# Attention scores in quarters of TensorE's array, and later places for the products behind them

## Chip, core and metric

One core of one Trainium2 chip runs the kernel alone. The metric is the device time of one execution in microseconds (us), taken as the median over runs. Engines are called by the profile's names: PE is TensorE's matmul, PEld its weight loads (they overlap PE), DVE is VectorE, ACT ScalarE, POOL GpSimd, SP SyncE, which starts most transfers.

## What is computed

Attention over pooled keys and values, then a mixture of experts on the rows that it gives. B = 8, H = 8, S = 576, D = 64; eight keys are pooled into one, so there are 72 pooled keys (SP in the kernel). The 4608 rows x of 512 go through a skip score, eight experts' gates and one expert each.

```python
k_p = k.reshape(B, H, Sp, pool, D).mean(axis=3)
v_p = v.reshape(B, H, Sp, pool, D).mean(axis=3)
scores = scale * np.matmul(q, k_p.transpose(0, 1, 3, 2))
scores = scores - np.max(scores, axis=-1, keepdims=True)
attn = np.exp(scores)
attn = attn / (np.sum(attn, axis=-1, keepdims=True) + 1e-09)
x = np.matmul(attn, v_p)            # then (B * S, H * D)
do_compute = x @ w_skip > 0         # other rows are left as x
e_idx = np.argmax(x @ w_gate, axis=1)
out = x + softmax(x @ w_gate)[e_idx] * (np.maximum(x @ w1[e_idx], 0) @ w2[e_idx])
```

## The kernel before

**Tiles.** The attention part takes 36 tiles (NT) of 128 tokens. All its matmuls are float32, and each shows as two instructions in the profile. A batch has four and a half tiles, so tiles 4, 13, 22 and 31 lie across two batches; they use matmuls on 64 output columns at a time, one half for each batch. Queries lie with two heads on the 128 partitions (64 dimensions each), so four head pairs make a tile. `scores` (L303) takes a pair's 128x128 block of queries as weights and streams 144 columns of `kbd`, a block-diagonal array: one head's 72 keys on the upper 64 partitions, the other's on the lower, zeros elsewhere. One half (two pairs, four heads) fills one bank of PSUM, `sc`.

**One iteration t** is a stage of a software pipeline over tiles, written out by hand; each engine works its instructions off in this order.

- ACT copies tile t−2's turned probabilities from PSUM (`turned_p`, L328, 128x640) and, where a new batch comes in, its turned pooled values (`turned_v`, L267).
- DVE normalises tile t−3 (`normal`: reciprocal L355, gates' part L359, rows L360, logits L362); the rows are stored by SP.
- PE computes the scores of tile t (L303). DVE takes the minimum of each head's (negated) scores (`softmax`, L309), ACT the eight exponentials (L315).
- With a new batch PE multiplies its turned values by the gates' weights (`gates_pe`, L278), and DVE spreads them over the arrays of values later in the iteration (`gates_dve`, L281, L284): so the value matmuls give the gates' logits beside the rows.
- PE runs route products if a group has them ready (`routes.products`, L397 to L401), then the values of tile t−2 (`values`, L341 and L344) into `o`, two banks that have one buffer, and turns tile t−1's exponentials (`turn_p`, L323, L324) into `pt`.
- DVE and ACT take further work from lists within a budget of time per iteration; POOL takes its own (sums of values, low halves of weights, memsets, and the table writes of routed groups, L415, one for each tile, an indirect transfer).

**Routing** goes in groups of 9, 5, 4, 6, 5, 4 and 3 tiles. A group's steps are a generator: DVE steps, ACT's exponentials (L394), PE's products, DVE's ranks and payments, then POOL's table writes. `routes.held` is set while a group stands before its exponentials or products.

**Behind the attention** PE goes on, from 147.0 us, with 128x512 and 128x384 matmuls of one expert's two layers on nine tiles of rows ("near" tokens: L532 to L534 for the first layer, L550 to L552 for the second). A list fixes PE's order there: 28 of the 32 steps of the first layer, then the transposes L1072 of rows that POOL gathers from the table (L1040) once all table writes are done, then the rest. Next comes the experts' part, in which PE is busy to the end.

```python
sc = [scores(t, i) for i in range(2)]
mn = softmax(t, sc)
if new is not None:
    gates_pe(new)
routes.products()
exponentials(t, sc, mn)
os_[t - 2] = values(t - 2, pts.pop(t - 2))
turn_p(es.pop(t - 1))
if new is not None:
    gates_dve(new)
```

## Time and profile before

| what | value |
|---|---|
| median of 3 runs | 480.49 us (479.95 to 480.7) |
| the profiled execution | 481.24 us, of which 479.2 us are the profile's span |
| granted clock of TensorE, mean | 0.999 |
| PE, PEld busy | 463.5 us, 417.1 us |
| DVE, ACT, POOL busy | 303.4 us, 225.7 us, 250.3 us |
| attention's last value matmuls on PE | 147.0 us |

The span runs from the first to the last instruction that the profile has; 2.04 us of the execution lie around it. Times within the trace count from the start of the span. Busy time is the sum of an engine's instructions, and a matmul's end is modelled, so that neighbours overlap. The granted clock is 1.00 where TensorE runs at 2.4 GHz and .50 where it runs at 1.2.

### The profile page before, as it was taken

What the parts mean: (1) busy time and instruction counts of PE and PEld (TensorE: products, weight loads), DVE (VectorE), ACT (ScalarE), POOL (GpSimd) and SP (SyncE); (2) the same over time, 40 slices, a digit from 0 to 9 for tenths busy, and PEclk for the clock granted to TensorE, in tenths of its full rate; (3) what the DMA queues carried; (4) which work ended last, traced back from release to release, by engine and by line L of the source; (5) the groups of instructions that cost most, each with busy time, mean ns of one, the idle gap of its engine ahead of it and who ended that gap; (6) DMA issues with size and microseconds to landing.
All of it is one profiled execution on the core that took longest, in us unless ns stands there. A gap on an engine that the chain in (4) does not pass through costs nothing. (4 is left out here: it accounts for less than half of the span.)

```text
span 479.2 us, 11182 instructions
## 1 busy us (share of the span) xinstructions
PE 463.5 (97%) x3043; PEld 417.1 (87%) x3044; DVE 303.4 (63%) x713; ACT 225.7 (47%) x578; POOL 250.3 (52%) x328
## 2 busy tenths in 40 slices
PE   7999999999999999899999999999999999999995
PEld 4799899989999979798989987989899898989894
DVE  5877888798788622578795667663846554343321
ACT  5678768888891211546462645612435251212110
POOL 4499499999998154363342424362624161515242
PEclk9999999999999999999999999999999999999999
DMA  8999999996931026679787497877687223322021
GB/s 278 388 396 390 361 352 332 384 333 207 328 122 68 11 62 215 230 228 308 247 289 244 136 290 241 300 240 251 202 256 262 89 95 101 129 66 88 22 88 42
DMA packets 52042, 103.88 MB, mean 217 GB/s; under 512 B 10031, under 2 KB 22959, under 8 KB 50336
## 3 DMA queue, kind: packets, MB, share of 16 engines
q1 hardware_dynamic: 40544, 78.18, 47.8%
q0 software_dynamic: 11456, 25.22, 15.0%
q8 instruction: 17, 0.28, 0.2%
q14 instruction: 25, 0.20, 0.1%
HBM read 80.85 MB, written 31.21 MB: 234 GB/s over the span
## 5 line engine op out<-in xcount | busy, mean ns | idle before, releaser
L1289 POOL DMA_INDIRECT out<-ring,slot x33 | 35.8, 1085 | 109.3 <-POOLq L1115 105.6
L315 ACT ACTIVATE e<-sc,mn 128x72 f32<-128x72 f32 x288 | 65.0, 345 | 7.4 <-DVE mn L309 6.8
L1527 ACT ACTIVATE hhi<-psl 128x256 fp32r<-128x256 f32 (+3 forms) x59 | 23.5, 400 | 94.0 <-ACTq L1115 93.5
L1384 PE MATMUL psl<-xlo,w1hi 128*128 128x256 f32 (+3 forms) x220 | 64.1, 291 | 0.0
L1383 PE MATMUL psl<-xhi,w1hi 128*128 128x256 f32 (+3 forms) x220 | 64.0, 291 | 0.0
L1385 PE MATMUL psl<-xhi,w1lo 128*128 128x256 f32 (+3 forms) x220 | 64.0, 291 | 0.0
L1284 POOL DMA_INDIRECT ring<-out,slot x42 | 46.6, 1109 | 22.6 <-issue 22.4
L341 PE MATMUL o<-vbd,pT 128*128 128x148 f32 (+1 forms) x312 | 49.4, 298 | 1.1 <-DVE x L360 1.1
L1626 DVE SCALAR_TENSOR_TENSOR hlo<-psl,hhi 128x256 fp32r<-128x256 f32 (+2 forms) x55 | 23.2, 423 | 41.3 <-DVEq L1115 39.0
L415 POOL DMA_INDIRECT table<-pay,r_di x36 | 36.7, 1018 | 12.6 <-DVE mb L443 6.4
L1383 PEld LDWEIGHTS psl<-xhi,w1hi 128*128 128x128 f32 x220 | 41.3, 188 | 0.8 <-issue 0.4
L1384 PEld LDWEIGHTS psl<-xlo,w1hi 128*128 128x128 f32 x220 | 41.3, 188 | 0.5
L341 PEld LDWEIGHTS o<-vbd,pT 128*128 128x128 f32 (+1 forms) x312 | 38.6, 179 | 3.6 <-ACT ring L213 1.0
L1385 PEld LDWEIGHTS psl<-xhi,w1lo 128*128 128x128 f32 x220 | 41.2, 187 | 0.0
L1297 POOL DMA_DIRECT2D sorted<-ring x39 | 22.2, 572 | 32.9 <-DMA ring<-out,slot 25.8
L1603 DVE TENSOR_TENSOR w2lo<-stage,w2hi 128x1024 fp32r<-128x1024 f32 x28 | 34.3, 1223 | 6.6 <-DVEq L1115 6.4
L1384 PE MATMUL psd<-xlo,w1hi 128*128 128x256 f32 (+3 forms) x132 | 38.4, 291 | 0.0
L1385 PE MATMUL psd<-xhi,w1lo 128*128 128x256 f32 (+3 forms) x132 | 38.4, 291 | 0.0
L1383 PE MATMUL psd<-xhi,w1hi 128*128 128x256 f32 (+3 forms) x132 | 38.4, 291 | 0.0
L1409 PE MATMUL mb<-w2hi,hlo 128*128 128x512 f32 x88 | 34.8, 396 | 0.0
L1409 PE MATMUL psf<-w2hi,hlo 128*128 128x512 f32 x88 | 34.8, 396 | 0.0
L1407 PE MATMUL psf<-w2hi,hhi 128*128 128x512 f32 x88 | 34.8, 395 | 0.0
(276 smaller groups left out, 1216.0 us busy)
## 6 DMA issues: line engine op xcount, KB each, us to landing
stage<-in_w SPq DMA_DIRECT2D x64, 512.0 KB, 5.5
sorted<-ring POOLq DMA_DIRECT2D x39, 256.0 KB, 3.3
out<-x SPq DMA_DIRECT2D x36, 256.0 KB, 5.4
stage<-in_k SPq DMA_DIRECT2D x6, 1152.0 KB, 8.8
blocks<-sorted SPq DMA_DIRECT2D x100, 64.0 KB
qt<-in_q SPq DMA_DIRECT2D x9, 512.0 KB, 7.4
hhi<-in_vm SPq DMA_DIRECT2D x4, 1024.0 KB, 7.7
hlo<-in_vm SPq DMA_DIRECT2D x3, 1024.0 KB, 9.8
```

Of the source, the lines that this page charges most:

```text
L315: nc.scalar.activation(ev[:, h // 2, k0:k0 + SP], sc[:, h * SP:(h + 1) * SP], AF.Exp, bias=mn[:, 4 * i + h:4 * i + h + 1], scale=-1.0)
L341: nc.tensor.matmul(o_[sl, g * 2 * VA:(g + 1) * 2 * VA], pT[:, 2 * a + g, sl], vbd[b % 2][:, 2 * a + g, :], start=(g == 0), stop=False)
L415: m = nc.gpsimd.indirect_dma_start(table, bass.IndirectOffsetOnAxis(ap=di[:, j:j + 1], axis=0), flat(fin["pays"][:, t0 + j:t0 + j + TW // ...
L1284: g.indirect_dma_start(ring[:, (s + 3) % 9, 0:D], None, out, bass.IndirectOffsetOnAxis(ap=slot[:, s:s + 1], axis=0), bounds_check=NTOK - 1 ...
L1289: g.indirect_dma_start(out, bass.IndirectOffsetOnAxis(ap=offsets, axis=0), ring[:, (s + 3) % 9, 0:D], None, bounds_check=NTOK - 1, oob_is_ ...
L1383: t.matmul(ps, whi[0][:, k, w], xhi[:, k, xs], start=(k == 0), stop=False)
L1384: t.matmul(ps, whi[0][:, k, w], xlo[:, k, xs], start=False, stop=False)
L1385: last = t.matmul(ps, wlo[0][:, k, w], xhi[:, k, xs], start=False, stop=(k == 3))
L1407: t.matmul(ps, hhi[:, k, sl], whi[1][:, k, :], start=(k == 0), stop=False)
L1409: last = t.matmul(ps, hlo[:, k, sl], whi[1][:, k, :], start=False, stop=(k == 7))
L1527: a.activation(hhi[:, f, xs], bank(f, xs, alone), AF.Relu).then_inc(sem["act"], 1)
L1603: v.tensor_tensor(chunk_of(wlo, c), chunk_view(stage[c], c), chunk_of(whi, c).bitcast(F32), ALU.subtract).then_inc(sem["wlo1" if c < 4 els ...
```

## The change

From tile 3 on the scores are computed in quarters: for each of four head pairs, each half of the tokens (64 weight columns) and each head (64 rows of the array) one matmul with 72 moving columns, 16 instead of 4 in the program (32 instructions in the profile instead of 8). The zeros of `kbd` are no longer read. The heads on the upper 64 rows go to one bank, those on the lower to the other; minimum and exponentials take the heads in that order. Tiles 0 to 2 keep the old form. The turned probabilities go to two banks and are copied in two instructions, 128x384 and 128x256. The gates' product on PE moves behind the values, and its spreading on DVE into the next iteration, ahead of the minimum. Route products that become ready in the iteration itself go behind the values from tile 15 on (PICKED), and DVE then takes one more route step instead of filling its budget; those that stood ready when the iteration began stay in front of the values. Of a group's last four DVE steps the two for payments now come before the two for ranks.

```diff
@@ scores, exponentials
-        def scores(t, half):
+        def by_halves(t):
+            return t < 3
+
+        def scores_by_halves(t, half):
             sc = ps_s.tile([128, 512], F32, name="sc")[:, 0:4 * SP]
             for g in range(2):
-                for sl, b in parts(t):
-                    nc.tensor.matmul(sc[sl, g * 2 * SP:(g + 1) * 2 * SP], qts[t // QG][:, t % QG, half * 2 + g, sl],
-                                     kbd[b % 2][:, half * 2 + g, :], start=True, stop=True)
+                nc.tensor.matmul(sc[:, g * 2 * SP:(g + 1) * 2 * SP], qts[t // QG][:, t % QG, half * 2 + g],
+                                 kbd[0][:, half * 2 + g, :], start=True, stop=True)
             return sc
 
+        def scores(t):
+            if by_halves(t):
+                return [scores_by_halves(t, i) for i in range(2)]
+            sc = [ps_s.tile([128, 512], F32, name="sc")[:, 0:4 * SP] for _ in range(2)]
+            for g in range(4):
+                for i, sl in enumerate(halves):
+                    b = (t * 128 + i * 64) // S
+                    for r, o in zip(halves, range(2)):
+                        nc.tensor.matmul(sc[o][sl, g * SP:(g + 1) * SP], qts[t // QG][r, t % QG, g, sl],
+                                         kbd[b % 2][r, g, o * SP:(o + 1) * SP], start=True, stop=True)
+            return sc
+
-        def exped(e, sc, mn, i):
-            ev = e[:, (4 * SP + GAP) * i:(4 * SP + GAP) * i + 4 * SP].rearrange("p (k g) -> p g k", g=2)
-            for h in range(4):
-                k0 = (h % 2 ^ i) * SP
-                nc.scalar.activation(ev[:, h // 2, k0:k0 + SP], sc[:, h * SP:(h + 1) * SP], AF.Exp,
-                                     bias=mn[:, 4 * i + h:4 * i + h + 1], scale=-1.0)
+        def exped(e, sc, mn, n, halved):
+            for j in range(4):
+                g, o = (2 * n + j // 2, j % 2) if halved else (j, n)
+                i = g // 2
+                ev = e[:, (4 * SP + GAP) * i:(4 * SP + GAP) * i + 4 * SP].rearrange("p (k g) -> p g k", g=2)
+                k0 = (o ^ i) * SP
+                nc.scalar.activation(ev[:, g % 2, k0:k0 + SP], sc[:, j * SP:(j + 1) * SP], AF.Exp,
+                                     bias=mn[:, 4 * n + j:4 * n + j + 1], scale=-1.0)
@@ turned probabilities
         def turn_p(e):
...
-                    nc.tensor.transpose(ptf[:, (2 * i + g) * 128:(2 * i + g) * 128 + 128], ev[:, g], ident)
-            nc.tensor.transpose(ptf[:, 512:640], e[:, 256:384], ident)
+                    nc.tensor.transpose(pt[:, i, (2 * i + g) * 128:(2 * i + g) * 128 + 128], ev[:, g], ident)
+                if i == 0:
+                    nc.tensor.transpose(pt[:, 0, 256:384], e[:, 256:384], ident)
 
         def turned_p():
-            pT = ap.tile([128, 5, 128], F32, name="pT")
-            nc.scalar.activation(flat(pT), ptf[:, 0:640], AF.Copy)
+            pT = [ap.tile([128, 3 - i, 128], F32, name=f"pT{i}") for i in range(2)]
+            for i, sl in enumerate((slice(0, 384), slice(256, 512))):
+                nc.scalar.activation(flat(pT[i]), pt[:, i, sl], AF.Copy)
             return pT
@@ values: the first half reads pT[0], the second pT[1] and the left columns pT[0]
-                        nc.tensor.matmul(o_[sl, g * 2 * VA:(g + 1) * 2 * VA], pT[:, 2 * a + g, sl], vbd[b % 2][:, 2 * a + g, :],
+                        nc.tensor.matmul(o_[sl, g * 2 * VA:(g + 1) * 2 * VA], pT[a][:, g, sl], vbd[b % 2][:, 2 * a + g, :],
...
-                    nc.tensor.matmul(ov[sl, :, 1, :], pT[:, 4, sl], vl4[b % 3][:, 2 * a:2 * a + 2, :], start=False, stop=True)
+                    nc.tensor.matmul(ov[sl, :, 1, :], pT[0][:, 2, sl], vl4[b % 3][:, 2 * a:2 * a + 2, :], start=False, stop=True)
@@ route
-            for a, b in zip(ranked, paid) if last else zip(paid, ranked):
+            for a, b in zip(ranked, paid) if last else (paid, ranked):
@@ Queue.products
             def products(self):
+                had = bool(self.held)
                 while self.held:
                     self.step(True)
+                return had
@@ the iteration
+            known = routes.held
             routes.exponentials()
             if t > 2:
                 normal(t - 3)
-                sc = [scores(t, i) for i in range(2)]
+                if t - 1 in turns:
+                    gates_dve(turns[t - 1])
+                sc = scores(t)
...
-            if new is not None:
-                gates_pe(new)
...
+            elif known or t < PICKED:
+                routes.products()
             else:
-                routes.products()
+                routes.exponentials()
             spent = act.take(t, 0.4 if new is not None else 0.0, 1)
             exponentials(t, sc, mn)
             os_[t - 2] = values(t - 2, pts.pop(t - 2))
+            if new is not None:
+                gates_pe(new)
+            fresh = t < NT - 1 and routes.products()
...
-            if new is not None:
-                gates_dve(new)
...
             while t < NT - 1 and busy < (DVE if t < PICKED else DVEL) and routes.step():
-                busy += 0.24
+                busy += 9 if fresh else 0.24
```

PE's order in the iteration of tile 9, the first of batch 2, before (`sc` scores, `o` values, `mb` gates, `pt` turned probabilities):

```order
L303 MATMUL sc<-ring,qt 128x144 x4
L278 MATMUL mb<-wgs,vT 128x36 x3
L341 MATMUL o<-vbd_121,pT 128x148 x2
L344 MATMUL o<-vl_123,pT 128x2x74
L341 MATMUL o<-vbd_121,pT 128x148 x2
L344 MATMUL o<-vl_123,pT 128x2x74
L323 MATMUL pt<-cfs,e_126 128x128 x4
L324 MATMUL pt<-cfs,e_126 128x128
```

and the same place in the change:

```order
L317 MATMUL sc<-ring,qt 64x72 x16
L359 MATMUL o<-vbd_121,pT_712 128x148 x2
L362 MATMUL o<-vl_123,pT_712 128x2x74
L359 MATMUL o<-vbd_121,pT_713 128x148 x2
L362 MATMUL o<-vl_123,pT_712 128x2x74
L278 MATMUL mb<-wgs,vT 128x36 x3
L339 MATMUL pt<-cfs,e_126 128x128 x2
L341 MATMUL pt<-cfs,e_126 128x128
L339 MATMUL pt<-cfs,e_126 128x128 x2
```

The gates' three matmuls stand behind the values, and the transpose of the left columns has moved to the middle of its five.

DVE's order at the entry of the same batch, before (`lg` logits, `mn` minimum, `vbd` and `vl` the spread gates, `kp` pooled keys, `rc` and `x` normalisation):

```order
L362 TENSOR_REDUCE lg<-l_635 128x9
L309 TENSOR_REDUCE mn<-sc 128x4 x2
L281 TENSOR_TENSOR vbd_120<-mb,cfs 128x8x9
L284 TENSOR_TENSOR vl_124<-mb,cfs 96x4x9
L208 TENSOR_REDUCE kp<-stage 128x72
L355 RECIPROCAL rc<-o 128x8
L359 TENSOR_TENSOR l_688<-o,rc 128x72
L360 TENSOR_TENSOR x<-o,rc 128x512
L362 TENSOR_REDUCE lg<-l_688 128x9
L309 TENSOR_REDUCE mn<-sc 128x4 x2
```

and in the change:

```order
L323 TENSOR_REDUCE mn<-sc 128x4 x2
L208 TENSOR_REDUCE kp<-stage 128x72
L373 RECIPROCAL rc<-o 128x8
L377 TENSOR_TENSOR l_784<-o,rc 128x72
L378 TENSOR_TENSOR x<-o,rc 128x512
L380 TENSOR_REDUCE lg<-l_784 128x9
L281 TENSOR_TENSOR vbd_120<-mb,cfs 128x8x9
L284 TENSOR_TENSOR vl_124<-mb,cfs 96x4x9
L323 TENSOR_REDUCE mn<-sc 128x4 x2
```

The two multiplications stand one normalisation later, directly ahead of the next tile's minimum. On POOL one memset and one table write change places; SP's order is the same.

## Rows read from the trace of the kernel before

**Rows 1.** The page: busy time, share of the span and instructions of each engine.
```profile
PE 463.5 (97%) x3043; PEld 417.1 (87%) x3044; DVE 303.4 (63%) x713; ACT 225.7 (47%) x578; POOL 250.3 (52%) x328
```

**Rows 2.** Busy us by stretch: stretch, length, PE, PEld, DVE, ACT, POOL (instructions), granted clock, DMA, GB/s.
```profile
17.00:55.70 38.70, 37.69 (x318) 35.59 (x318) 30.48 (x90) 29.15 (x107) 26.79 (x37) 1.00 1.02 393
55.70:156.00 100.30, 98.04 (x820) 92.58 (x819) 83.41 (x302) 75.30 (x252) 92.20 (x108) 1.00 0.76 266
```

**Rows 3.** Timeline of PE, 61 to 68 us: start, us, engine, line, operation, out<-in, count.
```profile
61.10 1.15 PE L303 MATMUL sc<-ring,xlo 128*128 128x144 f32 x8
62.15 0.74 PE L341 MATMUL o<-vbd,pT 128*128 128x148 f32 x4
...
63.74 0.63 PE L323 MATMUL pt<-cfs,e 128*128 128x128 f32 x4
...
64.31 1.15 PE L303 MATMUL sc<-ring,xlo 128*128 128x144 f32 x8
65.39 0.72 PE L341 MATMUL o<-vbd,pT 128*64 128x148 f32 x8
...
67.05 0.74 PE L323 MATMUL pt<-cfs,e 128*128 128x128 f32 x4
...
67.74 1.15 PE L303 MATMUL sc<-ring,qt 128*128 128x144 f32 x8
```

**Rows 4.** Weight loads of the scores by form: busy us, mean ns | idle before.
```profile
L303 PEld LDWEIGHTS sc<-ring,qt 128*128 128x128 f32 x160 | 21.1, 191 | 3.6 <-ACT ring L213 2.4 <-issue 1.0 <-ACT e L315 0.2
...
L303 PEld LDWEIGHTS sc<-ring,xlo 128*64 128x64 f32 x32 | 1.9, 136 | 0.3 <-issue 0.3
```

**Rows 5.** Timeline of one iteration; last, the turned values' copy by form.
```profile
78.65 0.63 PE L323 MATMUL pt<-cfs,e 128*128 128x128 f32 x4
...
79.26 0.68 DVE L360 TENSOR_TENSOR x<-o,rc 128x512 f32<-128x512 f32 x1
79.49 0.71 ACT L328 ACTIVATE pT<-pt 128x640 f32<-128x640 f32 x1 [1.21 <-PE pt L324]
...
80.61 1.80 ACT L315 ACTIVATE e<-sc,mn 128x72 f32<-128x72 f32 x8
...
L267 ACT ACTIVATE vT<-pt 128x384 f32<-128x384 f32 x8 | 3.9, 485 | 0.6 <-PE pt L262 0.6
```

**Rows 6.** Waits before gates' (L278) and route products (L397), us, times; DVE's gates (L281).
```profile
  ACT vT L267: 3.0, 7
...
  ACT ex L394: 1.7, 4
...
L281 DVE TENSOR_TENSOR vbd<-mb,cfs 128x72 f32<-128x72 f32 x8 | 1.9, 232 | 4.6 <-PE mb L278 2.8 <-ACT e L315 1.8
```

**Rows 7.** Timeline of POOL: first and last table write, gather [idle before <-releaser].
```profile
55.78 1.08 POOL L415 DMA_INDIRECT table<-pay,r_di  x1 [6.39 <-DVE mb L443]
...
155.03 0.98 POOL L415 DMA_INDIRECT table<-pay,r_di  x1 [0.30 <-issue]
158.10 1.08 POOL L1040 DMA_INDIRECT stage<-table,s_coli  x1 [2.08 <-DVE s_last L1060]
```

**Rows 8.** PE's transposes of the gathered rows (L1072), and the gather's landing.
```profile
162.82 0.34 PE L1072 MATMUL o<-cfs,stage 81*128 81x81 f32 x2
...
DMA to landing us min/median/max: 4.0/4.0/4.0
```

**Rows 9.** PE's 128x512 matmuls by form; the end of the span by stretch.
```profile
L739 PE MATMUL o<-ring 128*128 128x512 f32 x6 | 5.5, 1084 | 1.7 <-POOL ring L717 1.7
...
L817 PE MATMUL o<-ring 128*128 128x512 f32 x6 | 3.1, 593 | 0.0
...
L1394 PE MATMUL psf<-w2hi,hhi 128*128 128x512 f32 x8 | 3.3, 408 | 1.4 <-PEq L1115 1.4
...
474.00:476.00 2.00, 0.29 (x2) 0.00 (x0) 0.75 (x1) 0.00 (x0) 0.00 (x0) 1.00 0.12 45
478.00:479.20 1.20, 0.00 (x0) 0.00 (x0) 0.00 (x0) 0.00 (x0) 0.00 (x0) 0.54 0.34 128
```

More of the change, by code (lines that the diff above doesn't have):

```diff
@@ L258, in turn_v @@
         def turn_v(b):
-            tp = pt[:, 1, 128:512].rearrange("p (j n) -> p j n", j=3)
+            tp = ptf[:, 384:768].rearrange("p (j n) -> p j n", j=3)
             for j in range(2):
@@ L812, in exponentials @@
             es[t] = ebuf[t % 2]
-            for i in range(2):
-                exped(es[t], sc[i], mn, i)
+            for n in range(2):
+                exped(es[t], sc[n], mn, n, by_halves(t))
         def constant_product():
@@ L836, in attention @@
         gates_dve(0)
-        sc = [scores(2, i) for i in range(2)]
+        sc = scores(2)
         mn = softmax(2, sc)
@@ L855, in attention @@
                 normal(t - 3)
-                sc = [scores(t, i) for i in range(2)]
+                if t - 1 in turns:
+                    gates_dve(turns[t - 1])
+                sc = scores(t)
             if t == NT - 1:
```

## Prediction

> **What bounds the kernel now.** I read the page's first lines, then busy time by stretch, then single iterations in the timeline, then the waits of the lines that the change touches, and last the end of the attention part. TensorE (PE) works 97% of the span [rows 1]. In the attention part that share holds: 37.69 of 38.70 us while the pipeline fills, 98.04 of 100.30 us from 55.70 to 156.00 [rows 2]. So a tile costs what its matmuls cost: from the scores of one tile to those of the next pass 64.31 − 61.10 = 3.21 us [rows 3]. But the same stretch shows GpSimd (POOL) busy for 92.20 of 100.30 us, VectorE (DVE) for 83.41 [rows 2]: a second engine is nearly full, and PE's share alone doesn't tell what ends the part.
>
> **Scores in quarters.** Eight score instructions (each float32 matmul is two) take 1.15 us [rows 3]; I estimate the last one's length at .29, a quarter of it, so that starts lie (1.15 − .29) / 7 = .123 us apart and eight make .98 us of a tile. The quarters issue 32 instructions of 72 columns, which go to four places of the array. Columns beside each other are shown: in a boundary tile eight value instructions on 64 output columns take .72 us where four on 128 take .74 [rows 3], so two run at once. Row halves beside each other are in no row. If all four run at once, the 32 are 8 rounds of .123 / 2 = .061, or .49 us: .49 less per tile. Bounds: column halves only beside each other, 16 rounds, .98; nothing beside anything, 32, 1.95. Weight loads of 64 columns take 136 ns against 191 for 128 [rows 4], so 64 columns are worth 55 ns; if loads ran side by side in column halves only, 16 × .055 = .88 us, between these. I take .49: independent rows of the array ought to act as its independent columns do, and the row on columns is nearest.
>
> The array's shape now changes twice in every tile. The boundary tile that starts at 64.31 shows two changes, to value matmuls on halves and back to whole transposes: it lasts 67.74 − 64.31 = 3.43 us, .22 more than the plain one, and .11 of that lies in its four transposes, .74 us instead of .63 [rows 3]. I take +.22; the ends are 0, as part of it may be that tile's own, and twice that, .44, as a change of rows and columns at once is in no row.
> The Trainium skill, TensorEngine Tiling (Array Packing), section Key Properties, speaks against this change: a switch of the tiling mode, other than one between tiles of one mode, drains TensorE. The trace agrees in direction, with the .22 us above. Were the drain a whole instruction's estimated length, .29 us at either change, .36 us more a tile would be lost, and the gain below with it.
>
> A plain tile on PE is then 3.21 − .49 + .22 = 2.94 us, .27 less.
>
> **Loops that could hold it higher.** The output buffer is single: PE turns from a tile's values to its transposes at 78.65, and DVE has read the values for the last time by 79.26 + .68 = 79.94, 1.29 us later [rows 5]; then the next values may begin, which take 63.74 − 62.15 = 1.59 us [rows 3]: 2.88, and a few hundredths for the signal. ScalarE: the exponentials end at 80.61 + 1.80 = 82.41, 3.76 us behind 78.65; the first part of the copy (128x384 takes 485 ns as the row of the turned values shows [rows 5]) and the values, .48 + 1.59, close a loop of 5.84 us over two tiles, 2.92 each. In one piece the copy takes .71 [rows 5]; in two it should cost ScalarE .03 to .1 us more, which lies in its idle time, 25 of 100.3 us [rows 2]. Neither lies above PE's 2.94. Gain: .27 us in a plain tile; in the eleven or so of the 33 that carry most route steps I count nothing, as DVE is fullest there.
>
> **Moved work.** The gates' product waits .43 us for the turned values' copy, seven times, 3.0 in all [rows 6]; behind the values that copy is long done, so 3.0 goes. The gates' two DVE multiplications pass into the next iteration, between normalisation and the scores' minimum: the larger lasts .23 us [rows 6], and I estimate .4 for both. The minimum and the exponentials behind it wait for that, and through it for the gates' product, which is a tile old by then. Route products of late tiles stand behind the values, where the 1.59 us of the values covers ScalarE's exponentials; at most the 1.7 us that they waited for these in four places [rows 6] is there; I count nothing, as the early groups keep their place. The order of the two payment steps is worth nothing: both are DVE steps of the same length. Together PE's own work ends 22 tiles × .27 + 3.0 ≈ 9 us earlier (6 to 12).
>
> **What holds the end.** POOL's order doesn't change but for one swap of a memset with a table write. From its first table write at 55.78, for which it waited 6.39 us, to its last, 155.03 + .98 = 156.0, it is busy for 92.20 of 100.30 us [rows 2, 7]. It can't follow PE's 9 us. It moves only by what its first write moves: the route chain of the first group, which the program takes up behind tile 8 and ends some tiles later. Before that lie 7 plain tiles × .26 = 1.8 and two gates' waits, .8, less .4 for DVE's multiplications: 2.2 us (1 to 3.5). The gather behind the last write goes out at 158.10; the row puts its wait of 2.08 us down to a DVE step, but it reads what that write lands, so I let it move with POOL (were it DVE's alone, it would gain more, inside the bound of 6 below). It lands 4.0 us later, 162.1, and PE's transposes of it stand at 162.82 [rows 7, 8], in PE's fixed order behind 28 of 32 steps of the first layer: .7 us of slack there today, of which I count .6. With PE 9 us earlier and the gather 2.2, PE stands before these transposes: they come 2.2 + .6 = 2.8 us earlier, and PE idles 9 − 2.8 ≈ 6 us. Behind them PE is busy to the end, so 2.8 is what reaches the time.
>
> **The clock.** A PE that idles for 6 us is in no row of the middle of the program. At its end the last matmul is over by 474.3, the granted clock is 1.00 from 474.00 to 476.00 and .54 from 478.00 to 479.20 [rows 9]: behind a PE at rest the clock had fallen to the lower of its levels, 1.2 of 2.4 GHz. A gap of 1.40 us left it high: the instructions behind it took 408 ns, as elsewhere [rows 9]. At the lower level the first six 128x512 instructions took 1084 ns against 593 for six of the same form later [rows 9]: 5.5 us in all, of which 5.5 × (1 − 593 / 1084) = 2.5 us were lost to the clock. I take that as the price of a fall; the ends are 0, if PE's gap comes in pieces, and twice that, 5.0, as a fall in mid-program is in no row.
> The Trainium skill, TensorE: Matmul & The Clock Gate, section Why this matters for your kernels, warns of idle gaps between bursts of matmuls: the clock goes back to its lower level. The rows agree at the end of the span; no row here shows such a gap with work behind it.
>
> **Sum.** The profiled execution took 481.24 us, .75 above the median of the runs. 481.24 − 2.8 + 2.5 = 480.9, in the median's terms **480.2**; with the bounds of both terms (gain 1.6 to 6, if some of POOL's 8.1 idle us goes too, loss 0 to 5.0) 474.5 to 483.9.
>
> **Rivals.**
> - *The clock stays high.* PE's gap is shorter, or broken by steps that become ready. For it: 9 is an upper guess of PE's gain, DVE has 83.41 us in the stretch. Then 481.24 − 2.8 − .75 = 477.7. Chance .22.
> - *Row halves don't run beside each other* (slower). Place: scores of every tile from the third. PE's gain of 9 us is .27 a tile over 33 tiles; with the .6 of slack the change breaks even where scores and shape changes cost .29 more than the .71 I take, 1.00 us a tile. With column halves only, .98 + .22 = 1.20: .20 × 33 = 6.6 us later, about 487; with nothing beside anything 1.95 + .22 = 2.17: 1.17 × 33 = 38.6, about 519. For it: no row shows row halves at once. Against: by the diff the two row halves read different partitions and write different banks, so they share nothing that column halves don't. Chance .12, mostly the first.
> - *POOL gives way.* Its 92.20 us hold spans that are rough, and its work between table writes may shrink. Then PE's 9 us come through: 481.24 − 9 − .75 = 471.5. Chance .07.
> - *The change does nothing for a tile.* DVE with 83.41 of 100.30 us, its minimum now behind two more multiplications, holds the tile at 3.2. Only the gates' waits go: the gather comes .8 − .4 = .4 us earlier, and with .6 of slack that is 1.0 us in all; PE then idles 3.0 − 1.0 = 2.0 us, nearer to the 1.40 that left the clock high: 481.24 − 1.0 − .75 = 479.5. Chance .13.
>
> **Chances and range.** The forecast has .46. A measurement of this kernel tells .2%, .96 us, from no change: below 479.53 is faster, above 481.45 slower. Of the forecast's .46 I put .17 on faster, .21 on same and .08 on slower, as its loss to the clock lies below or above 2.5; with .22 and .07 on faster, .13 halved between faster and same, and .12 on slower, with .03 from same to slower for steps that DVE delays: faster .52, same .25, slower .23. The range leaves out the rivals on row halves and on POOL giving way, .19 together: it goes from 475.0 to 483.0, a little inside the sum's own bounds, since both would have to come at once.
>
> **What would show it.** Score instructions of a tile starting four at a time, .06 apart in rounds, and some .5 to .7 us from the first to the values; the plain tile's period near 2.9; no wait of the gates' product; transposes after scores at .74; POOL's first table write near 53.6 and its last near 153.8; PE idle for some 6 us ahead of the gather's transposes at about 160.0, and a granted clock near .5 behind them for about 5 us. A period of 3.4 or more would make the forecast wrong at the row halves; a gather that lands before PE gets there, at POOL; a granted clock of 1.00 through the gap, at the clock.

## The result, and the profile after

In the set of runs on which the prediction was put on record the change is slower: 484.03 us as the median of 20 runs (480.84 to 490.82), against 480.66 for the kernel before on the same chip (20 runs), a ratio of 1.0053 with a 95% interval of 1.0027 to 1.0078. The ratios leave disturbed runs out (five of the 20 here), so they aren't the ratios of the medians. The forecast was 480.2, with 475 to 483 and most of the chance on faster. The same program was timed in three more sets of runs, each beside the kernel before:

| set | the change | the kernel before | ratio, 95% interval | minima held behind POOL's indirect transfers (below) |
|---|---|---|---|---|
| first | 484.03 (20 runs) | 480.66 | 1.0053 [1.0027, 1.0078] | 7 tiles |
| r1_after | 483.21 (10) | 480.59 | 1.0062 [1.0014, 1.0109] | 7 tiles |
| k1_after | 479.37 (12) | 479.82 | 0.9990 [0.9967, 1.0012] | none |
| m1_after | 485.95 (11) | 480.2 | 1.0090 [1.0056, 1.0124] | 7 tiles |

So the change is slower in three sets and can't be told from the kernel before in one. The sets ran on different chips or at different times, and the last column, which comes from the traces, goes with the sign.

The page's first part and busy time by stretch in the first profile of the change (span 480.3 us, execution 482.39), as [rows 1, 2] have them for the kernel before:

```profile
PE 455.9 (95%) x3803; PEld 406.1 (85%) x3804; DVE 301.0 (63%) x713; ACT 228.0 (47%) x614; POOL 251.6 (52%) x328
```
```profile
55.70:156.00 100.30, 89.93 (x1316) 82.18 (x1306) 78.56 (x285) 75.49 (x273) 89.37 (x106) 1.00 0.75 265
```

PE is busy 89.93 us where it was busy 98.04, 8.11 us less: that is near the 9 us that the prediction took off PE. But PE's idle time in the stretch rose by the same 8.11 us, from 2.26 to 10.37, and the attention ended later: the first matmuls behind it start at 148.40 us, where they started at 147.0.

The timeline of PE at the boundary tile of [rows 3], which starts with the scores at 62.74, and then at a plain tile (start, us, engine, line, operation, out<-in, array's shape, operands, count):

```profile
62.74 0.73 PE L317 MATMUL sc<-ring,xlo 64*64 64x72 f32 x32
63.50 0.72 PE L359 MATMUL o<-vbd,pT 128*64 128x148 f32 x8
...
80.94 0.39 PE L339 MATMUL pt<-cfs,e 128*128 128x128 f32 x2
...
81.61 0.73 PE L317 MATMUL sc<-ring,xhi 64*64 64x72 f32 x32
82.38 0.74 PE L359 MATMUL o<-vbd,pT 128*128 128x148 f32 x4
...
83.96 0.39 PE L339 MATMUL pt<-cfs,e 128*128 128x128 f32 x2
```

The 32 score instructions take .73 us. In the boundary tile the values follow .76 us behind their start (62.74 to 63.50), where it was 65.39 − 64.31 = 1.08 [rows 3]; in the plain tile .77 us (81.61 to 82.38), where it was 62.15 − 61.10 = 1.05. Where PE waits for nothing, a plain tile takes 83.96 − 80.94 = 3.02 us from transposes to transposes, .19 less than the 3.21 before.

What VectorE's minima (L323) waited for (us in total, times), in the change's first profile, and below it for the minima of the kernel before (L309):

```profile
  PE sc L317: 13.1, 14
...
who waited for it (us, times):
  ACT e L331: 14.9, 20
```
```profile
  PE sc L303: 3.4, 8
...
who waited for it (us, times):
  ACT e L315: 6.8, 12
```

VectorE waits for scores 13.1 us instead of 3.4, and ScalarE's exponentials wait for the minima 14.9 instead of 6.8. These waits grew by about what PE's idle time grew; that they cause it isn't shown by the sums. Last, POOL's first and last table write, which answer to [rows 7], and PE at the transposes of the gathered rows, which answer to [rows 8]:

```profile
54.28 1.09 POOL L433 DMA_INDIRECT table<-pay,r_di  x1 [6.69 <-DVE mb L461]
...
156.02 0.98 POOL L433 DMA_INDIRECT table<-pay,r_di  x1 [0.30 <-issue]
```
```profile
164.03 0.34 PE L552 MATMUL sc<-xhi,w1lo 128*128 128x384 f32 x1
164.22 0.34 PE L1096 MATMUL o<-cfs,stage 81*128 81x81 f32 x2
```

POOL writes its first table row 1.50 us earlier and its last one 1.0 us later than before. PE comes to the transposes at 164.22 without a gap ahead of them. The wait of 6 us that the forecast had there doesn't exist, nor does a fall of the clock behind it (granted clock 1.00 from 164 to 168 us).

### The profile page after: what moved, and what is told of

Its sections match the earlier page's. It is cut to its first block, busy times and chain, and to the rows that moved or that the text cites. A ratio compares the mean times of both kernels' runs of the same rounds, so it can differ in the third digit from the quotient of the medians.

```text
span 480.3 us, 12750 instructions
## 1 busy us (share of the span) xinstructions
PE 455.9 (95%) x3803; PEld 406.1 (85%) x3804; DVE 301.0 (63%) x713; ACT 228.0 (47%) x614; POOL 251.6 (52%) x328
## 3 DMA queue, kind: packets, MB, share of 16 engines
q0 software_dynamic: 11456, 25.22, 14.9%
## 5 line engine op out<-in xcount | busy, mean ns | idle before, releaser
L1313 POOL DMA_INDIRECT out<-ring,slot x33 | 37.7, 1143 | 122.0 <-POOLq L1139 119.2
L331 ACT ACTIVATE e<-sc,mn 128x72 f32<-128x72 f32 x288 | 65.2, 347 | 15.6 <-DVE mn L323 14.9
L323 DVE TENSOR_REDUCE mn<-sc 128x4 f32<-128x288 f32 x72 | 29.7, 451 | 15.8 <-PE sc L317 13.1
```

What stands on the lines that cost most here:

```text
L323: nc.vector.tensor_reduce(mn[:, i * 4:i * 4 + 4], sc.rearrange("p (h k) -> p h k", k=SP), axis=AX.X, op=ALU.min)
L331: nc.scalar.activation(ev[:, g % 2, k0:k0 + SP], sc[:, j * SP:(j + 1) * SP], AF.Exp, bias=mn[:, 4 * n + j:4 * n + j + 1], scale=-1.0)
L1313: g.indirect_dma_start(out, bass.IndirectOffsetOnAxis(ap=offsets, axis=0), ring[:, (s + 3) % 9, 0:D], None, bounds_check=NTOK - 1, oob_is_ ...
```

## Experiments

### The parts of the change

Each of these three takes one part out of the change or puts one alone into the kernel before; they ran on one chip.

**e1_halves**: all of the change, with the scores in the old halves.

```diff
         def by_halves(t):
-            return t < 3
+            return True
```

> All of the change but its quarters: every tile's scores by halves, as before. Theory H: what the change lost is the completion signal of the 64x64 score matmuls, which the minimum on VectorE gets some 1.1 us late whenever the scores end inside one of GpSimd's indirect table writes (seven of seven such tiles in the changed kernel's trace, none elsewhere). Then no minimum starts over .3 us behind its scores with VectorE idle, its waits for the scores fall from 13.1 us to 2 to 3, and the time is 479.5 to 480.7, the same as the kernel before or a little less, with a granted clock of .998 or more in every run. Rival R: the later places of gates, products and route steps and the two copies cost what the quarters gain. Then this kernel is slower than the changed one: 484 or more.

Measured: 480.8 us against 480.38, ratio 1.0010 [0.9993, 1.0027]. The moved gates and route products, with the copy in two parts, give nothing by themselves. The gates' product no longer waits for the turned values, as foreseen, but the tile that gains hands it back in the next one: the values of the tile at index 16 start 1.49 us earlier than in the kernel before, those of the next .42. The timeline of DVE and PE there shows who takes it:

```profile
77.17 0.75 PE L278 MATMUL mb<-wgs,vT 128*128 128x36 f32 x6
...
78.03 0.21 DVE L426 TENSOR_REDUCE mb<-ex 128x5 f32<-128x45 f32 x1 [1.73 <-PE mb L278]
...
79.83 0.74 PE L360 MATMUL o<-vbd,pT 128*128 128x148 f32 x4 [0.29 <-DVE x L379]
...
80.03 0.81 DVE L324 TENSOR_REDUCE mn<-sc 128x4 f32<-128x288 f32 x2
```

The route's payment step (L426) writes the same PSUM tile `mb` as the gates' product (L278). In the new order the product stands before it, behind the values, and the step waits 1.73 us for it. The normalisation is queued behind the payment on DVE, so PE's next values wait for `x`; and the two spreads L281 and L284 stand ahead of the minimum. The waits of L426 for L278 come to 3.5 us, two of them, in this trace. The prediction asked what the spreading holds up, and of the payment steps it said that their order is worth nothing.

**e2_quarters**: the kernel before with the quarters alone, that is with `scores` and `exped` as the change has them.

```diff
-                sc = [scores(t, i) for i in range(2)]
+                sc = scores(t)
```

> The kernel before with the quarters alone: gates, products, route steps and the single copy of turned probabilities stay as they were. Theory H: minima held for about 1.1 us in 6 to 10 tiles, waits of the minimum for the scores 8 us or more, time 481 to 485, and runs with granted clocks below .995 among them. Rival R: few or no held minima, and 475 to 479.

Measured: 481.63, ratio 1.0044 [1.0011, 1.0077]. The plain tile keeps its period of 3.21 us: PE waits for ScalarE's copy instead.

```profile
PE o L357 <- ACT pT L344: 3.4, 15, 0.4
PE o L357 <- DVE x L376: 3.2, 3, 1.3
```

The copy in one piece ends behind the shorter scores (3.4 us in 15 waits), so the quarters need the copy in two; the prediction had named that loop, with the first part's .48 us in it.

**e3_rows**: the change, with the array's rows halved and the columns whole.

```diff
-                for i, sl in enumerate(halves):
-                    b = (t * 128 + i * 64) // S
+                for sl, b in parts(t):
```

> The change with row halves only: 64 rows by all 128 token columns, 8 matmuls (16 instructions) of 72 columns a tile, column halves only in the four boundary tiles. If two row halves run at once, 8 rounds of .061 us make the same .5 us as the quarters with half the instructions, and the plain tile stays at 3.0 us. Theory H, in the form that row halves bring the hold: minima held as in the change, time 481 to 485. In the form that column halves bring it: held in boundary tiles only, time 476 to 480. Rival R expects the time of the change, 482 to 485, and no held minima.

Measured: 487.06, ratio 1.0132 [1.0111, 1.0153]. The scores of a plain tile by timeline, and the weight loads of the scores by form, row halves and then the quarters that its boundary tiles keep:

```profile
64.42 1.11 PE L316 MATMUL sc<-ring,xlo 64*128 64x72 f32 x16
```
```profile
L316 PEld LDWEIGHTS sc<-ring,xlo 64*128 64x128 f32 x96 | 5.8, 187 | 0.7
...
L316 PEld LDWEIGHTS sc<-ring,xlo 64*64 64x64 f32 x64 | 1.5, 132 | 0.7 <-issue 0.7
```

Row halves run beside each other, two at once, and gain next to nothing: 16 instructions are 8 rounds, .11 us apart, and take 1.11 us where whole-array scores take 1.15 [rows 3]. Halving the streamed columns alone thus took a round only from .123 us to .11, with loads of 128 columns as before (187 and 191 ns); in quarters, with loads of 64 columns (132 ns), a round is .0625. I conclude that a round goes with its load; no run changes the load alone. The rival on row halves was wrong: they do run beside each other.

### What holds the minima

**e4_memset**: POOL's table writes replaced by memsets.

```diff
-                m = nc.gpsimd.indirect_dma_start(table, bass.IndirectOffsetOnAxis(ap=di[:, j:j + 1], axis=0),
...
+                for _ in range(6):
+                    nc.gpsimd.memset(fin["none"], NO_TOKEN)
```

> The change with each of the 36 indirect table writes of GpSimd replaced by six small memsets of about the same length (about 1 us). The table stays empty, so the experts find no tokens and the output rows are left as x; only the attention part of the trace is compared. Theory H: no minimum starts over .3 us behind its scores while VectorE idles; the waits of the minimum for the scores fall from 13.1 us to 3 or less, and the last value matmuls on TensorE come 4 us or more earlier than in the changed kernel (148.7 us there). Rival: the minimum waits for something else on TensorE (the values or products behind the scores), and the held minima stay, 6 or more of them.

Measured in one run: a span of 489.6 us. It tells nothing of the change, since this kernel leaves the routing table empty, and the memsets end late, so that PE stands 9.8 us before the gather's transposes. In the attention the last value matmul starts at 146.47, 1.65 us earlier than the change's 148.12, and the minima wait 6.5 us for scores instead of 13.1. Both fall short of what was expected. So the table writes have part of those waits. This is how it looks in the change's first profile, and in its third (k1_after), at one and the same tile:

```profile
84.63 0.73 PE L317 MATMUL sc<-ring,xhi 64*64 64x72 f32 x32
...
85.12 0.99 POOL L433 DMA_INDIRECT table<-pay,r_di  x1 [0.17 <-issue]
...
85.38 0.74 PE L359 MATMUL o<-vbd,pT 128*128 128x148 f32 x4
...
86.61 0.33 SPq L292 DMA_DIRECT2D xhi<-in_q  x1
86.65 0.82 DVE L323 TENSOR_REDUCE mn<-sc 128x4 f32<-128x288 f32 x2 [1.12 <-PE sc L317]
```
```profile
84.54 0.73 PE L317 MATMUL sc<-ring,xhi 64*64 64x72 f32 x32
...
85.09 0.99 POOL L433 DMA_INDIRECT table<-pay,r_di  x1 [0.17 <-issue]
...
85.47 0.82 DVE L323 TENSOR_REDUCE mn<-sc 128x4 f32<-128x288 f32 x2
...
85.87 0.39 SPq L292 DMA_DIRECT2D xhi<-in_q  x1
```

In both the scores end inside a table write (85.36 and 85.27). Below, the minimum starts at 85.47, while the write is still on. Above, it starts at 86.65, .54 us behind the write's end at 86.11, with DVE idle for 1.12 us, and SP's load of queries, which waits for the same scores, goes out no earlier than 86.61; PE itself has long gone on to the values. The trace also records when the semaphore that the minimum waits for was raised by the scores: at 86.56 and 86.60 above, at 85.38 below. So it is PE's signal that comes late, and not DVE that is slow to start. I call such a minimum held: it starts .38 to .65 us behind the end of an indirect transfer of POOL inside or just ahead of which its scores ended, with DVE idle. The change's first profile has held minima in the tiles 15, 18, 21, 22, 24, 30 and 34; six stand behind table writes, that of tile 30 behind another indirect transfer of POOL (L512, rows of `out` into `ring`).

**g1_gates, g2_signal, g4_qp, g5_all** ran together on another chip: the change with its gates at the old places (g1); the change with two tiny whole-array matmuls behind each tile's quarters, for which the minima then wait (g2); the kernel before with quarters and two copies alone (g4); and g4 with the tiny matmuls (g5).

```diff
@@ g2, g5: behind the quarters
+            for f in full if t > 7 else ():
+                nc.tensor.matmul(f[:, 4 * SP:4 * SP + 8], c["ones"], c["ones"][:, 0:8], start=True, stop=True)
@@ g1, g4, g5: gates
+            if new is not None:
+                gates_pe(new)
...
             os_[t - 2] = values(t - 2, pts.pop(t - 2))
-            if new is not None:
-                gates_pe(new)
```

> The change with the gates' product and its spreading at their old places (behind the scores, and in the same iteration). Theory G: the move gains nothing, because VectorE's payment steps of a route, which write the same PSUM tile as the gates' product, stand behind that product in order and now wait up to 1.7 us for it, so that the tile behind each new batch loses the .9 to 1.5 us that the new batch's tile gains. Then that wait (3.5 us in two places with scores by halves) falls below 1 us, the tile with the new batch is about 1 us longer and the next one about 1 us shorter than in the change, the last value matmuls come within 1 us of the change's 148.1, and the time is 481 to 485. Rival: the move was worth its 3 us, and this kernel's last values come at 150 or later, time 485 or more.

> The change with two very small matmuls of the whole array's shape behind the quarters, one into spare columns of each scores bank, from tile 8 on; the minimum then waits for these instead of for the last quarters. They cost .1 to .2 us a tile. Theory Ha: what is held while GpSimd issues an indirect transfer is the signal that the 64x64 matmuls themselves give, so no minimum is held, the last values come 1 to 2 us before the change's 148.1, and the time is 480 to 482.5. Theory Hb: TensorE's signals are held behind such matmuls whatever gives them; then 5 or more minima start .3 us or more late, as in the change.

> The kernel before with the quarters and the copy in two parts alone; gates, products, route steps and payments as before. With the quarters alone the tile period stayed at 3.21 us, because the values wait for the single copy. Theory: the two copies let the values start .2 us earlier, a plain tile takes 3.0 us, minima are still held in 5 to 9 tiles, the last values come at 146 to 149, and the time is 480 to 484. Rival: the tile period stays at 3.2 us, as something else than the copy holds it.

> The same with the small whole-shape matmuls behind the quarters (from tile 8). If held signals are what eats the gain: no held minima, plain tiles of 3.05 to 3.1 us, last values at 143.5 to 146, three us or more before the change's; then GpSimd's chain of table writes is the next limit (first write about 55, last about 154), TensorE waits at most 2 us for the gathered rows, and the time is 477.5 to 480. If something else holds the tiles, 480 to 482.

Measured, against 480.04: g1 481.97, ratio 1.0038 [1.0001, 1.0075]; g2 481.56, 1.0036 [1.0015, 1.0056]; g4 480.89, 1.0014 [0.9991, 1.0037]; g5 481.36, 1.0047 [1.0018, 1.0075]. No minimum was held in any of the four, with the tiny matmuls or without: 4 to 8 tiles in g1, g2 and g5, and one in g4, started their minimum while a write was on. In all four a product of DVE took 2.2 to 3.1 us instead of .68; that has its own part below. The last value matmul starts at 149.49 (g1), 152.18 (g2), 149.44 (g4) and 146.76 (g5), so it can come later than the change's 148.12 without any held minimum. So the set tells nothing of a remedy, and leaves open whether the moved gates or the chip make the difference to the change's own trace.

**r1_after, r2_quarters** put the change and the quarters alone on a further chip.

> The changed kernel as it is, once more. In its first trace every minimum whose scores ended inside an indirect table write of GpSimd started .4 to .6 us behind the end of that write; in the runs with the gates at their old place none did. Theory H1: the hold belongs to this kernel's order (gates and products behind the values): then 5 or more minima are held again. Theory H2: it belongs to the chip or the execution: then it may be gone here, and with it some of the waits of the minimum (13.1 us before). Time 481.5 to 485 either way.

> The quarters alone, once more, beside the run before on the same chip. H1 doesn't name this kernel (its gates are at the old place, and its minima were held in 6 tiles); H2: held here if and only if the changed kernel's are held in this call.

Measured, against 480.59: r1 483.21, ratio 1.0062 [1.0014, 1.0109], with the same seven held tiles but for one (16 for 15); r2, one run, 480.83, held in three.

**k1_after, k2_gates, k3_qp** are the change, g1 and g4 again, side by side in one set.

> The change again, beside the next three on one chip. Theory A (the late minima belong to a stretch in which quarters end inside a table write, whatever the rest of the kernel): late minima in 6 or more tiles here and in k2 and k3 too, and all three within 1 us of each other. Theory B (they come with the change's own timing, that is with its moved gates): late minima here in 6 or more tiles, last value matmul near 148.1 us; in k2 and k3 none; median 482 to 483.5, some 2 us above k3. Theory C (the chip decides): the number of late minima is the same in all three, none or many.

> The change with gates' product and spreading at their old places. Theory A: like k1, within 1 us. Theory B: 1 to 2.5 us below k1, no late minima; if VectorE's low product stretches, its trace shows a PE wait of over 1 us for the normalisation near 102 to 106 us. Theory C: as k1 in late minima.

> The kernel before with quarters and two copies alone. If the stretched low products take its gain (as the run with memsets in their place had it, 479.35), then here 480 to 481, against before 480.3: the values of tile 20 start 1 to 1.6 us earlier than before's, and a low product of 2 us or more gives that back. Rival: the gain comes through and it is 479.0 to 479.8, below before.

Measured, against 479.82: k1 479.37, ratio 0.9990 [0.9967, 1.0012]; k2 480.83, 1.0025 [0.9994, 1.0056]; k3 479.52, 0.9991 [0.9966, 1.0015]. No minimum held in any of them. The change itself runs here without one (its minima wait 5.8 us for scores, not 13.1), and its last value matmul starts at 146.10 instead of 148.12 or, in r1, 148.27. So it is not the moved gates: what decides goes with the set of runs, and r1 and k1 even carry the same chip number.

**m1_after, m2_signal** put the change and g2 side by side once more.

> The change once more. Theory A (late minima cost the 2 to 3 us): if six or more minima start over .35 us behind a table write that ended after their scores, with VectorE idle, then the last value matmul is near 148.2 us and the median 2.5 to 3.5 us above before's; if none does, it is near 146.1 and the median within 1 us of before's. Rival (something else makes the sets differ): the median doesn't follow the late minima.

> The change with two tiny whole-array matmuls behind each tile's quarters from tile 8, for which the minima wait. They cost about .1 to .2 us a tile, 3 to 5 us in all, if nothing else changes. If m1 has late minima and the lateness is in the quarters' own signal: none here, and the time is at most 1.5 us above m1's. If the lateness is in VectorE or in any signal of TensorE: as many late minima here as in m1, and 3 us or more above m1. If m1 has none: none here, and 1 to 3 us above m1.

Measured, against 480.2: m1 485.95, ratio 1.0090 [1.0056, 1.0124]; m2 482.23, 1.0041 [1.0016, 1.0067]. Here minima are held again, the same seven in m1; the last value matmul starts at 149.14. And they are held in m2 too, in six tiles, though the minimum there waits for a whole-array matmul that starts behind the quarters. One of them:

```profile
63.63 0.73 PE L318 MATMUL sc<-ring,xlo 64*64 64x72 f32 x32
63.78 0.99 POOL L436 DMA_INDIRECT table<-pay,r_di  x1 [0.17 <-issue]
...
64.30 0.20 PE L321 MATMUL sc<-ones 128*128 128x8 bf16 x2
...
65.40 0.82 DVE L326 TENSOR_REDUCE mn<-sc 128x4 f32<-128x288 f32 x2 [0.96 <-PE sc L321]
```

So the lateness is not that of the quarters' own signal alone; either a later signal of PE can't overtake it, or it arises elsewhere. That m2 came out below m1 isn't explained by its held minima, which are about as many; m1's runs had the lower granted clock, .987 to 1.0 against .993 to .999. Over all sets there are 16 profiles of kernels with quarters or row halves and with table writes: in the sets with held minima all eight of these have some, in the two sets without none of eight has. Halves, in the sets with held minima, show none: in e1_halves a minimum starts .73 us ahead of a write's end, at the end of its scores. And e3_rows has both kinds in one trace, first a boundary tile in quarters, then a plain tile in row halves:

```profile
94.27 1.09 PE L316 MATMUL sc<-ring,xlo 64*64 64x72 f32 x32
...
94.52 0.99 POOL L432 DMA_INDIRECT table<-pay,r_di  x1 [0.17 <-issue]
...
96.05 0.46 DVE L322 TENSOR_REDUCE mn<-sc 128x4 f32<-128x288 f32 x1 [1.31 <-PE sc L316]
```
```profile
143.41 1.11 PE L316 MATMUL sc<-ring,qt 64*128 64x72 f32 x16
...
143.93 0.99 POOL L432 DMA_INDIRECT table<-pay,r_di  x1 [0.16 <-issue]
...
144.63 0.82 DVE L322 TENSOR_REDUCE mn<-sc 128x4 f32<-128x288 f32 x2 [1.03 <-PE sc L316]
```

The quarters' minimum is held, .54 us behind the write's end at 95.51. That of the row halves starts .11 us behind its scores, with the write still on; so does that of tile 17. One minimum of row halves (tile 20), whose scores end .10 us behind a write, comes .42 behind the write's end. So the hold goes with the quarters; of the row halves one is late.

### What took the rest

**h1_qp_nolow, h2_before_nolow**: g4, and the kernel before, with DVE's five products of the weights' low halves (L607, in the kernel before L589) replaced by memsets of zero.

```diff
-  dve.add(now["t"] + 1, now["t"] + 2, 0.65, lambda: low_v(cc, i))
+  dve.add(now["t"] + 1, now["t"] + 2, 0.65, lambda: nc.vector.memset(piece(wlo, cc, i).bitcast(F32), 0.0))
```

> Quarters and the two copies alone (480.89 us before), with the five products on VectorE that make low halves of weights during the attention replaced by a memset to zero: the experts' first expert loses the low parts of five pieces, a little of its precision. In that kernel's trace two of these products took 2.8 and 2.7 us instead of .68, while GpSimd ran tensor operations, TensorE waited 4.2 us behind them, and its granted clock fell to .50 for 3.5 us. Theory P (the two engines get in each other's way at SBUF, and TensorE's gap costs its clock): no DVE instruction of the attention over 1.5 us, no granted clock under .9 between 20 and 160 us, last value matmuls at 143.5 to 146 (149.4 there), and 477 to 479.3. Rival: the gap comes from elsewhere, and the time stays at 480 to 482.

> The kernel before with the same five products replaced by memsets. There the stretched products are 1.84 and 1.16 us long and TensorE waited .8 us for one. Theory P: 0 to 1.5 us faster than the kernel before, 479 to 480.4; the difference of the quarters and copies beside it is then 1 to 2.5 us in their favour.

Measured, against 480.59: h1 479.35, ratio 0.9963 [0.9927, 0.9999]; h2 479.52, 0.9992 [0.9970, 1.0013]. The reason for the two is in g4's timeline, of DVE, then POOL, then PE:

```profile
101.46 2.82 DVE L607 TENSOR_TENSOR w1lo<-stage,w1hi 128x512 fp32r<-128x512 f32 x1
```
```profile
101.87 0.63 POOL L254 TENSOR_TENSOR ring<-ls,cfs 96x256 f32<-96x256 f32 x1
102.44 1.28 POOL L603 TENSOR_TENSOR w1lo<-stage,w1hi 128x512 fp32r<-128x512 f32 x1
```
```profile
105.40 1.33 PE L359 MATMUL o<-vbd,pT 128*128 128x148 f32 x4 [2.48 <-DVE x L378]
```

A product of .68 us elsewhere takes 2.82 where POOL runs two tensor operations beside it; the normalisation behind it is late, and PE waits 2.48 us. Up to there g4 was 1.64 us ahead of the kernel before (values at index 23), at index 27 it is 2.81 behind. Without these products (h1) the values are 1.3 to 1.8 us ahead of it from index 24 to 33, with three held minima. That explains g4's late values; a gain of the quarters and copies isn't shown by it, since the kernel before without the products (h2) comes to 479.52 against h1's 479.35, and the two intervals overlap.

The Trainium skill, SBUF — State Buffer, section Who interferes with whom, has the mechanism: a VectorE operation with two inputs in SBUF contends with a GpSimd operation that reads SBUF, since its second input comes through a read interface that the two share. The trace agrees: L607 has two such inputs, POOL's L254 and L603 read SBUF beside it, and the product takes 2.82 us instead of .68; the interface itself shows in no trace.

**k4_qp_later**: k3, with those products one iteration later.

```diff
-  dve.add(now["t"] + 1, now["t"] + 2, 0.65, lambda: low_v(cc, i))
+  dve.add(min(now["t"] + 2, NT - 2), min(now["t"] + 3, NT - 1), 0.65, lambda: low_v(cc, i))
```

> k3 with VectorE's low products one iteration later. If their meeting with GpSimd's tensor operations is what costs, and one iteration parts them: longest low product in the attention .7 to 1.3 us, 0.5 to 1.5 us below k3, and below before: 478.8 to 479.7. Rival 1: GpSimd's tensor operations stand in each iteration, so they meet all the same (a product of 2 us or more in the trace) and the time is k3's within .5 us. Rival 2: a later low product meets the weights' next load or the first layer of the last part, which waits: slower than k3.

Measured: 484.8, ratio 1.0084 [1.0056, 1.0112]. The products shrink to .68 to 1.36 us, but one of them now waits 4.18 us for a load of weights into `stage`, and PE waits behind it:

```profile
PE mb L278 <- DVE mb L400: 4.2, 1, 4.2
```

The second rival was right: the place was moved onto the next load. So no complete version was found that surely beats the kernel before; k3 and g4 stand at 0.9991 and 1.0014.

## Why the prediction was wrong

**Scores in quarters: right, with the gain a little too large.** Four run at once; .77 us to the values is .28 less than 1.05. The terms were .49 for the scores and .22 back for the changes of shape, .27 net a tile; measured .19 (3.21 to 3.02). What the changes of shape cost is in that difference, and .22 was too small for it by at most .08.

**The step that failed is "PE's own work ends 9 us earlier", and with it "what bounds the kernel".** PE's busy time in the stretch did fall by 8.11 us, but busy time is not an end: the last value matmul starts at 146.69 in the kernel before, at 148.12 in the change, and at 146.10, .59 earlier, even in k1_after, where no minimum is held. The prediction worked out two loops, of the output buffer (2.88 us) and of ScalarE (2.92), and found PE's 2.94 above both. It took DVE's part in them from one iteration [rows 5], and left out DVE's other work as a link. PE's waits in the kernel before and, below it, in k1_after (us in total, times, longest):

```profile
PE o L341 <- DVE x L360: 1.1, 2, 0.8
```
```profile
PE o L359 <- DVE x L378: 5.8, 7, 1.7
PE mb L415 <- ACT ex L412: 2.2, 3, 1.1
```

So the loop of the output buffer, through DVE's normalisation, is the one that holds PE most there, 5.8 us instead of 1.1. DVE's own start didn't move either. In halves the first minimum can start after half of the scores; in quarters both wait for all of them. From the first score to the first minimum, where DVE is free, it is .76 us before (from 67.74 [rows 3]) and .85 after (from 81.61):

```profile
68.50 0.88 DVE L309 TENSOR_REDUCE mn<-sc 128x4 f32<-128x288 f32 x2
```
```profile
82.46 0.82 DVE L323 TENSOR_REDUCE mn<-sc 128x4 f32<-128x288 f32 x2
```

The scores got shorter, and what hangs on them got no earlier. My reading is that PE's 97% had covered a chain that runs once a tile through all engines (scores, minimum, exponentials, turning, copy, values, normalisation) and was nearly as long as PE's work; the waits agree with it, but no run shortens the chain alone. The rival "the change does nothing for a tile" named DVE and had .13.

**The gates: wrong.** "3.0 goes" held on PE, but the product moved in front of a payment step that shares its PSUM tile, and 3.5 us of waits came back on DVE (e1_halves: 1.0010).

**POOL as the next bound and the clock behind a 6 us gap: not tested by the change**, as PE never got ahead: its last table write came at 156.02 (forecast 153.8), and no wait stood before L1096. In k3_qp, whose attention ends earliest of the kernels with all their work, the last value matmul starts 1.41 us ahead of the kernel before (145.28) and the last table write 1.09 us ahead (153.94), so that far POOL followed PE. Only e4_memset, with POOL's work made longer, showed such a gap, and there the clock did as forecast:

```profile
163.30:173.00 9.70, 0.00 (x0) 0.00 (x0) 0.00 (x0) 0.47 (x1) 4.86 (x19) 0.75 0.04 11
173.00:178.00 5.00, 4.95 (x16) 4.88 (x17) 1.39 (x5) 0.48 (x1) 0.00 (x0) 0.50 0.02 3
```

Behind PE's 9.8 us of rest the granted clock is .50, the lower level (1.2 GHz), for the next 5 us of work; half of it, 2.5 us, I estimate as lost. That is the price that the prediction took from the first six instructions (L739), though the trace records no granted clock before 7.1 us, so that their level was inferred. The clock was a real term in another place, too. In m1_after it fell behind a stretch in which PE, behind the held minimum of tile 34, worked 1.71 of 3.00 us; the mean then is .55, most of it at the lower level:

```profile
138.00:141.00 3.00, 1.71 (x38) 1.30 (x36) 2.17 (x7) 3.00 (x12) 2.67 (x5) 1.00 0.50 181
141.00:144.00 3.00, 2.79 (x12) 2.79 (x13) 2.53 (x10) 2.00 (x8) 2.80 (x4) 0.55 0.09 26
```

The mean granted clock of the change's runs lies between .984 and 1.0, and its time between 480.8 and 490.8 in the first set, the longest times with the lowest clocks (.984 to .989 above 488 us); the runs of the kernel before beside the later sets have .992 to 1.0.

**What goes with the loss** are the held minima. With them the attention's last value matmul starts at 148.12 to 149.14, without them at 146.10, on the same program: 2.0 to 3.0 us. Beside the kernel before the medians of the four sets give −.45 us without them and +2.6 to +5.8 with them; I put the part above 3.0 down to the lower clock. That they go together is shown on four sets; that nothing else differs between the sets is not. One thing does: PE's wait ahead of L1418, behind the attention, is 1.57 us at 204.71 in the change's first profile and is missing there in k1_after, so that it and the 2.0 us make up nearly all of the 3.7 between the two spans (480.3 and 476.6). The kernel before has 1.40 of it too [rows 9]; what makes it come and go stays open. The forecast's 480.2 lies near the one set without held minima, for reasons that were not the forecast's.

## What to carry to other kernels

An engine at 97% can hide a chain behind it: before its time is cut, walk one whole iteration through every engine, and ask of each link whether it starts earlier, not whether the engine has less to do. A product moved to save its own wait may become the wait of what shares its buffer; look for every later writer of the tile that it writes. And a change that is sensitive to when another engine's transfers run should be timed in several sets of runs before it is kept: here one chip gave both outcomes.

## What the runs showed of the hardware

- With scores in 64x64 quarters, signals from PE that fall into or just ahead of an indirect transfer of POOL reach DVE and SP only .38 to .65 us behind its end in some sets of runs, and at once in others, for one and the same program. A whole-array matmul behind the quarters doesn't help. With row halves two of three such minima of one trace started at once, with whole-array scores all. What sets the one or the other stays open.
- Four 64x64 quarters start within about .02 us of each other, in rounds of .0625 us, weight loads included (132 ns each); row halves with 128-column loads in rounds of .11.
- A VectorE product of two SBUF operands, .68 us elsewhere, took up to 3.2 us (e3_rows) where GpSimd tensor operations ran beside it.
